# Wider pieces in the conversion of the weights, and softmax chains shared by two token tiles, in a fused attention and soft mixture kernel

## Chip, cores and metric

The kernel runs on one core of one Trainium2 chip. The metric is the device time of one execution in microseconds (us); lower is better. The engines are named as the profile names them: PE (TensorE; its weight loads are a row of their own, PEld), DVE (VectorE), ACT (ScalarE), POOL (GpSimd) and SP, which here only issues DMAs.

## What is computed

Three stages follow each other: an attention with a window of 32 and 32 global tokens, a dense two layer block, and a soft mixture of eight experts.

```
attn_out = attention(q_l, k_l, v_l, q_g, k_g, v_g)     # 4 batches, 8 heads, 512 + 32 rows, 64 wide
x = attn_out.transpose(0, 2, 1, 3).reshape(2176, 512)
h = x @ w_in                                           # 512 x 2048
g = maximum(0.01 * h, h)
x = g @ w_out                                          # 2048 x 512
logits = x @ phi                                       # 512 x 32
d = exp(logits - logits.max(0));  d /= d.sum(0)        # over the tokens
slot_in = d.T @ x
slot_out = per expert: maximum(slot_in @ w1, 0) @ w2
c = exp(logits - logits.max(1));  c /= c.sum(1)        # over the 32 slots
out = c @ slot_out
```

w_in and w_out come as 64 bit floats, so the kernel reads them as pairs of 32 bit words and makes 32 bit floats of them itself.

## The kernel before

The 2176 rows are 17 token tiles of 128 (16 of the local rows, the last of the global ones). x @ w_out is never formed: the kernel makes pmat = w_out @ phi once, so that a tile's logits are g @ pmat, and sums d.T @ g over the tiles (`uacc`); w_out is applied to that sum at the end.

**The conversion.** `w_items` goes through w_in in 16 pieces of 128 x 512 (four column blocks f, four row blocks k), `p_items` through w_out in 16 pieces (c, j). `Stream` keeps raw loads ahead of their use: `fetch` issues a load of 128 x 256 word pairs into a ring of seven buffers, `next` converts the oldest half piece and lets the next load follow. The loads are issued by SP, in order with all its other loads. One `convert` is five instructions: two on ACT (L248 for the high words, L249 for the low ones), two on DVE (L251, L255), and an add on POOL (L259), each 128 x 256, so ten for a piece. A piece of w_in is then split in two parts for the matmuls, by ACT (L307) and by POOL or DVE (L308); its high words pass through PSUM for f > 0 (`cv`). A piece of w_out, in one of four buffers `wo` that w_in's pieces share, is stored to HBM as converted (L337, `wo_f`), and transposed on PE (`chunk`, L344); ACT copies that (L346), and after four chunks `prod` (L353) adds the block's part of pmat. The first nine half pieces of w_out have slots of their own (`spread`, in the attention's tags se, eT and kw); the rest use the ring.

**The token tiles.** `b_H(t, f)` is one 512 column block of h for tile t: 12 matmuls (L688) and an ACT instruction that makes g (L695). Blocks of tiles 0 to 2 run while the weights are converted (`hs`), those of tile 3 (`h3`) after that. Then comes, per tile, the softmax chain that `l_items` lists: transposes of g (`b_L`, L725, evacuated at L727), the logits (`b_M`, L739), their copy (L748), a matmul that brings the four partial sums together (L754), the running maximum (L758, L762), the exponentials (L763), the rescaling of the running sum (L767 to L769), a transpose (L799), the row softmax (`d_rows`, L786 to L794) and the sum over tokens (`u_add`, L809, L814). Each step needs the one before it, and goes from PE to DVE to ACT and back.

**The order.** The statements near L989 run the chain of tile 2, then `merge` lays the chains of tiles 0 and 1 and the rest of tile 3's blocks among the attention of batch 1 (`s4` to `s7`) by the weights beside each item. The chain of tile 3 is laid among the blocks of tile 4 by `b_items`. When the kernel is built, a scheduler orders the instructions of each engine once more; each engine then runs its list in order. From tile 4 on, `b_items` alternates blocks and chains, and the last two tiles have one joint chain (`j_D`) on 256 columns.

## Time and profile before

| what | value |
|---|---|
| median of 3 runs | 515.6 us (515.17 to 520.35) |
| profiled execution | 517.65 us |
| its span | 515.7 us |
| PE busy | 469.5 us (91%) |
| DVE, ACT, POOL busy | 282.1, 240.5, 166.2 us |
| granted PE clock, mean | 0.973 |
| moved by DMA | 90.26 MB, 175 GB/s over the span |

The span is the time from the first to the last recorded instruction; the execution's own time has some 2 us more around it. All stretches and durations below come from this one execution, which took 2.05 us more than the median. "PE busy" holds pipelined matmuls, so a stretch at 91% still has waits in it, and the idle time before an instruction stands apart with what ended it.

### The profile page before, as it was taken

To read this page: it belongs to the slowest core of one execution; us is meant where nothing else is said; L and a number is where in the kernel's file an instruction comes from. 1 tells how busy PE (TensorE), PEld (TensorE's weight loads), DVE (VectorE), ACT (ScalarE), POOL (GpSimd) and SP (SyncE) were. 2 spreads that over 40 slices of the span, in tenths; PEclk is the share of its full clock that TensorE was granted. 3 is DMA by queue.
4 is the path that set the end of the run, shared out by engine and by line. 5 is a ranking of instruction groups with operands and counts; after the bars stand their busy time and mean duration, and the time that the engine had idled before them with its cause. 6 is when DMAs were issued, how large, how long until landed. Compare 5 with 4: busy or idle time off the path is not lost.

```text
span 515.7 us, 13708 instructions
## 1 busy us (share of the span) xinstructions
PE 469.5 (91%) x5327; PEld 324.7 (63%) x5327; DVE 282.1 (55%) x956; ACT 240.5 (47%) x742; POOL 166.2 (32%) x309
## 2 busy tenths in 40 slices
PE   8867798868998979999999979999999999999993
PEld 5645575546775756666767657778677777633353
DVE  4585868659658476565453646534755531312422
ACT  4676888758845345444154254324433442300222
POOL 2044787453301113406233251406666620000000
PEclk9987899997999999999999999999999999999997
DMA  9989679598867471532431203209820059999977
GB/s 173 198 203 242 194 211 335 171 316 251 185 156 151 128 147 25 104 75 76 104 70 35 56 1 57 85 19 394 324 81 2 1 197 344 377 384 378 304 236 209
DMA packets 122397, 90.26 MB, mean 175 GB/s; under 512 B 75804, under 2 KB 101212, under 8 KB 122332
## 3 DMA queue, kind: packets, MB, share of 16 engines
q1 hardware_dynamic: 119660, 88.33, 60.4%
q10 hardware_dynamic: 2672, 1.05, 0.8%
q8 instruction: 42, 0.69, 0.6%
q14 instruction: 23, 0.19, 0.1%
HBM read 76.68 MB, written 8.65 MB: 165 GB/s over the span
## 4 chain that ended last, share of the span: by engine, by line
PE 65%; DMA 14%; DVE 8%; ACT 7%; issue 2%; SPq 2%; POOL 1%; ACTq 0%; DVEq 0%; POOLq 0%
PE hp L688 32%; PE ehp L1177 3%; PE up L809 3%; DMA rraw<-in_moe_w_in_dram 3%; PE po L492 3%; PE sc L433 3%; PE lg L739 2%; DMA vw<-vw 2%; PE gtp L725 2%; DMA rraw<-in_moe_w_out_dram 2%; ACT se L453 2%; DMA vw<-in_v_l_dram 2%; PE etp L472 2%; PE sop L1253 1%; DMA qk<-in_q_l_dram 1%
## 5 line engine op out<-in xcount | busy, mean ns | idle before, releaser
L688 PE MATMUL hp<-wi,xxh 128*128 128x512 f32 x512 | 167.0, 407 | 4.0 <-ACT g L695 2.6
L688 PEld LDWEIGHTS hp<-wi,xxh 128*128 128x128 f32 x512 | 91.9, 190 | 34.8 <-issue 10.6
L716 POOL COPY g<-gb 32x256 f32<-32x256 f32 x206 | 82.5, 400 | 79.3 <-DVE gb L707 66.6
L688 PE MATMUL hp<-wi,xxl 128*128 128x512 f32 x256 | 100.8, 395 | 0.0
L695 ACT ACTIVATE g<-hp 128x512 f32<-128x512 f32 x60 | 35.2, 592 | 66.3 <-PE hp L688 64.4
L453 ACT ACTIVATE se<-se,nmx 128x128 f32<-128x128 f32 x128 | 49.6, 391 | 21.6 <-DVE nmx L451 18.8
L688 PEld LDWEIGHTS hp<-wi,xxl 128*128 128x128 f32 x256 | 48.4, 189 | 11.8 <-issue 0.8
L200 POOL COPY vw<-vw 32x1664 f32<-32x1664 f32 x10 | 15.7, 1574 | 97.7 <-DMA vw<-in_v_g_dram 68.3
L259 POOL TENSOR_TENSOR wn<-wn,rraw 128x256 int32<-128x256 int32 x32 | 26.2, 834 | 37.0 <-DMA rraw<-in_moe_w_in_dram 25.5
L707 DVE STREAM_TRANSPOSE gb<-g 128x512 f32<-128x512 f32 x32 | 22.4, 705 | 23.0 <-ACT g L695 17.7
L445 DVE CUSTOM_DVE_ANT_0 se<-sc,mask 128x128 f32<-128x128 f32 x128 | 28.9, 284 | 7.1 <-PE sc L433 6.9
L433 PE MATMUL sc<-kw,qT 64*32 64x128 f32 x1024 | 29.7, 284 | 0.5 <-DVE kw L404 0.3
L492 PE MATMUL po<-vw,eT 128*32 128x64 f32 x1024 | 23.7, 228 | 6.2 <-DMA vw<-vw 4.7
L259 POOL TENSOR_TENSOR wo<-wo,rraw 128x256 int32<-128x256 int32 x23 | 18.5, 818 | 26.6 <-DMA wo_f<-wo 4.9
L492 PEld LDWEIGHTS po<-vw,eT 128*32 128x32 f32 x1024 | 18.1, 113 | 13.5 <-issue 10.6
L472 PE MATMUL etp<-identr,se 128*128 128x128 f32 x128 | 22.3, 296 | 4.6 <-ACT gT L727 3.3
L249 ACT ACTIVATE rraw<-rraw 128x256 int32<-128x256 uint32 x55 | 23.3, 433 | 5.8 <-DMA rraw<-in_moe_w_in_dram 4.9
L433 PEld LDWEIGHTS sc<-kw,qT 64*32 64x32 f32 x1024 | 19.4, 109 | 8.1 <-issue 4.4
L453 ACT ACTIVATION_READ_ACCUMULATOR se<-se,nmx 128x1 f32 x128 | 24.3, 189 | 0.0
L476 DVE COPY eT<-etp 128x512 f32<-128x512 f32 x28 | 18.8, 686 | 7.0 <-PE etp L472 6.7
L404 DVE COPY kw<-kT 128x672 f32<-128x672 f32 x32 | 19.0, 631 | 5.3 <-ACT kT L393 5.2
L472 PEld LDWEIGHTS etp<-identr,se 128*128 128x128 f32 x128 | 15.3, 148 | 10.3 <-ACT gT L727 4.0
(227 smaller groups left out, 803.3 us busy)
## 6 DMA issues: line engine op xcount, KB each, us to landing
ew<-in_moe_w_dram SPq DMA_DIRECT2D x23, 1024.0 KB, 8.5
rraw<-in_moe_w_in_dram SPq DMA_DIRECT2D x32, 256.0 KB, 3.5
vw<-in_v_l_dram SPq DMA_DIRECT2D x60, 112.0 KB, 3.6
rraw<-in_moe_w_out_dram SPq DMA_DIRECT2D x23, 256.0 KB, 5.3
ew<-in_moe_w_dram SPq DMA_DIRECT2D x9, 512.0 KB, 9.1
ew<-in_moe_w_dram SPq DMA_DIRECT2D x17, 256.0 KB, 5.2
wo_f<-wo SPq DMA_DIRECT2D x16, 256.0 KB, 3.8
vn<-in_v_l_dram SPq DMA_DIRECT2D x4, 1024.0 KB, 6.4
```

The source lines that it names most:

```text
L249: nc.scalar.activation(out=m, in_=lo, func=AF.Copy, scale=2.0 ** -29)
L259: nc.gpsimd.tensor_tensor(out=di, in0=di, in1=m, op=ALU.add)
L404: nc.vector.tensor_copy(kw[:, :, 0:96], src)
L433: last_a[0] = nc.tensor.matmul(bks[e][32 * u:32 * u + 32, P * T:P * T + P], qt[64 * e:64 * e + 64, 32 * U:32 * U + 32], kw[win(U) // (NW / ...
L445: nc.vector.tensor_tensor_reduce(out=s[:, T, :], in0=bk[:, P * T:P * T + P], in1=mask[:, 0 if T == 0 else 2 if T == NT - 1 else 1, :], sca ...
L453: exp_last[0] = nc.scalar.activation(out=s[:, T, :], in_=s[:, T, :], func=AF.Exp, bias=nmx[:, e, T:T + 1], accum_out=sm[:, T, e:e + 1],).ins
L472: last_a[0] = nc.tensor.transpose(pt[:, P * T:P * T + P], es[e][:, T, :], ident).ins
L492: last_a[0] = nc.tensor.matmul(pov[32 * u:32 * u + 32, T, e, :], ets[e][:, 32 * U:32 * U + 32], vw[:, win(U), e, :], start=True, stop=True ...
L688: nc.tensor.matmul(hp, a[:, k, :], w[c][:, k, :], start=(k == 0 and n == 0), stop=(k == KD - 1 and n == 2),)
L695: nc.scalar.activation(out=gs, in_=hp, func=AF.Prelu, alpha=0.01)
L707: nc.vector.transpose(out=gb[:, f % 2], in_=gs)
L716: copy(dst[32 * c:32 * c + 32, :, a], src[32 * a:32 * a + 32, :, c])
```

## The change

1. Raw words are loaded and converted in pieces of 128 x 512. The ring has four buffers of that width in place of seven of half of it; the first eight half pieces of w_out (c = 0) stay 256 wide, in eight slots of their own in place of nine. The shared `wo` buffers become three in place of four, which pays for the larger ring.
2. The chains of tiles 2 and 0, and of tiles 1 and 3, are joined (`pair_items`): the logits of both tiles stand side by side, and the copy, the sum of the parts, the maximum, the exponentials and the rescaling run once on 256 columns. `d_rows` still runs once for each tile; the sums over tokens of both tiles are added up in PSUM and added to `uacc` once.
3. The order around it: the pair (2, 0) is laid among block 2 of tile 3 and the first step of `s5`; the pair (1, 3) and block 3 of tile 3 among the rest of the attention of batch 1. Tile 4's blocks then have no chain among them.

```diff
@@ -225,7 +225,9 @@
 
     raw_last = [None]
 
-    def fetch(pool, src, tag="raw", bufs=7):
+    RING = 4
+
+    def fetch(pool, src, tag="raw", bufs=RING):
         n = src.shape[1]
         raw = pool.tile([P, n] + ([2] if src.dtype == U32 else []), src.dtype, tag=tag, name=tag[:1] + "raw", bufs=bufs)
         raw_last[0] = nc.sync.dma_start(out=raw, in_=src).ins
@@ -277,7 +279,7 @@
 
         def next(self, dst=None, half=None):
             self.start()
-            self.ahead = max(self.ahead - 1, 7) if self.ahead > 7 else self.ahead
+            self.ahead = max(self.ahead - 1, RING)
             r = convert(self.pool, self.raw.pop(0), dst, half)
             return r
 
@@ -290,20 +292,18 @@
     def w_items():
         items = []
         win_s = Stream(st, [
-            w_in_s[P * k:P * k + P, 512 * f + 256 * h:512 * f + 256 * h + 256]
-            for f in range(NQ) for k in range(KD) for h in range(2)
-        ], 7)
+            w_in_s[P * k:P * k + P, 512 * f:512 * f + 512]
+            for f in range(NQ) for k in range(KD)
+        ], RING)
         items.append((0.0, win_s.start))
 
         def piece(f, k):
             if k == 0:
                 wi[f] = [wp.tile([P, KD, 512], F32R, tag="w", name="wi") for _ in range(2)]
             t, tlo = wi[f]
-            w = pb.tile([P, 512], F32, tag="wo", name="wn", bufs=4)
+            w = pb.tile([P, 512], F32, tag="wo", name="wn", bufs=3)
             cv = bank("sc", "cv", 2) if f else None
-            for h in range(2):
-                c = slice(256 * h, 256 * h + 256)
-                win_s.next(w[:, c], cv[:, c] if f else None)
+            win_s.next(w, cv)
             nc.scalar.copy(t[:, k], w)
             (nc.vector if f and k % 2 else nc.gpsimd).tensor_tensor(out=tlo[:, k], in0=w, in1=t[:, k], op=ALU.subtract)
 
@@ -317,12 +317,13 @@
         items = []
         wts = {}
         wout_s = Stream(st, [
-            w_out_s[512 * j + P * c:512 * j + P * c + P, 256 * h:256 * h + 256]
-            for c in range(4) for j in range(4) for h in range(2)
-        ], 7)
+            w_out_s[512 * j + P * c:512 * j + P * c + P, a:z]
+            for c in range(4) for j in range(4)
+            for a, z in (((0, 256), (256, 512)) if c == 0 else ((0, 512),))
+        ], RING)
         def begin():
             with tc.issue_after(raw_last[0]):
-                wout_s.spread([("se", 4)] * 4 + [("eT", 2)] * 2 + [("kw", 3)] * 3)
+                wout_s.spread([("se", 4)] * 4 + [("eT", 2)] * 2 + [("kw", 3)] * 2)
                 wout_s.start()
 
         items.append((0.0, begin))
@@ -330,9 +331,9 @@
         wos = []
 
         def conv_(c, j):
-            wo = pb.tile([P, 512], F32, tag="wo", name="wo", bufs=4)
-            for h in range(2):
-                wout_s.next(wo[:, 256 * h:256 * h + 256])
+            wo = pb.tile([P, 512], F32, tag="wo", name="wo", bufs=3)
+            for h in range(2) if c == 0 else (None,):
+                wout_s.next(wo if h is None else wo[:, 256 * h:256 * h + 256])
             if wo_f is not w_out:
                 nc.sync.dma_start(out=wo_f[512 * j + P * c:512 * j + P * c + P, :], in_=wo)
             wos.append(wo)
@@ -875,6 +876,48 @@
             (1.0, lambda: b_U(t)),
         ]
 
+    def p_M(ts, i):
+
+        if i == 0:
+            ms["M"] = bank("sm", "lg", 1)
+        lg = ms["M"]
+        for f in range(NQ):
+            gT = lst.pop((ts[i], f))
+            for c in range(4):
+                nc.tensor.matmul(
+                    lg[32 * c:32 * c + 32, P * i:P * i + P], pmat[:, c, f, :], gT[:, c, :],
+                    start=(f == 0), stop=(f == NQ - 1), skip_group_check=True,
+                )
+
+    def p_D1(ts):
+        lp = sb.tile([P, 2 * P], F32, tag="lp", name="lp", bufs=1)
+        nc.vector.tensor_copy(lp, ms["M"][:, 0:2 * P])
+        ms["lp"] = lp
+
+    def p_D2(ts):
+        ms["st"] = d_cols(ms["M"][:, 2 * P:4 * P], ms["lp"])
+
+    def p_D3(ts):
+        lg = ms["M"]
+        for i, t in enumerate(ts):
+            nc.tensor.transpose(lg[:, P * i:P * i + P], ms["st"][:, P * i:P * i + P], ident)
+        ms["ds"] = [(d_rows(t, lg[:, P * i:P * i + 64]), gt.pop(t)) for i, t in enumerate(ts)]
+
+    def pair_items(ts):
+        its = []
+        for i, t in enumerate(ts):
+            its += [
+                (0.9, lambda t=t: (b_L(t, 0), b_L(t, 1))),
+                (0.9, lambda t=t: (b_L(t, 2), b_L(t, 3))),
+                (0.6, lambda i=i: p_M(ts, i)),
+            ]
+        return its + [
+            (0.1, lambda: p_D1(ts)),
+            (0.5, lambda: p_D2(ts)),
+            (0.5, lambda: p_D3(ts)),
+            (2.0, lambda: u_add(ms["ds"], ts[-1])),
+        ]
+
     def h_items(t):
         its = [(2.6, lambda f=f: b_H(t, f)) for f in range(NQ)]
         if t + 1 < NTT:
@@ -899,6 +942,9 @@
             li = l_items(t - 1)
             h = [held((1.3, lambda t=t, f=f, a=a: b_H(t, f, a))) for f in range(NQ) for a in range(2)]
             x = [(0.5, lambda t=t: b_X(t + 1), t + 1)] if t + 1 < NTT else []
+            if t == NT:
+                its += h[0:4] + x + h[4:]
+                continue
             if t - 1 in BLK:
                 its += h[0:2] + [li[1]] + h[2:4] + [li[2]] + x + [behind(h[4])]
                 its += [li[3]] + [behind(x) for x in h[5:8]] + [li[4], li[5]]
@@ -986,11 +1032,9 @@
     xb.append(bctx.enter_context(tc.tile_pool(name="xb", bufs=1, side="right")))
     gctx = ExitStack()
     gp.append(gctx.enter_context(tc.tile_pool(name="gp", bufs=1, side="right")))
-    for x in l_items(2):
-        x[1]()
+    merge(pair_items((2, 0)), [h3[2]] + s5[:1])
     load_v(NP + 1)
-    l0, l1 = l_items(0), l_items(1)
-    merge(l0 + h3[2:] + l1, s4[-1:] + s5 + s6 + s7)
+    merge(h3[3:] + pair_items((1, 3)), s4[-1:] + s5[1:] + s6 + s7)
     b_X(NT)
     attn = [None] + [sum((step(n) for n in range(NP * b, NP * b + NP)), []) for b in range(2, B)]
     LB = NTT - 2
```

What the build makes of it stands at three places.

SP's list around the fourth load of values (`vw`; L231 and L233 are the raw loads, L184 and L185 the copies of a window of values within SBUF). Before:

```order
L598 DMA gn<-in_q_g_dram 32x8x64 x4
L962 DMA phis<-in_moe_phi_dram 128x4x32
L231 DMA rraw<-in_moe_w_in_dram 128x512 x3
L184 DMA vw<-vw 32x1792 x2
L185 DMA vw<-vw 32x13x128
```

And now:

```order
L599 DMA gn<-in_q_g_dram 32x8x64 x4
L1008 DMA phis<-in_moe_phi_dram 128x4x32
L233 DMA rraw<-in_moe_w_in_dram 128x1024
L184 DMA vw<-vw 32x1792 x2
L185 DMA vw<-vw 32x13x128
```

One raw load of twice the width stands ahead of the copies, where there were three.

ACT's list at the first pieces of w_out that reuse a `wo` buffer (sraw, eraw, kraw and rraw are raw words; g and wt are evacuations of PE's results). The semaphores DMAHW5 and DMAHW6 before, and DMAHW1 and DMAHW2 now, are those of the first and second store to `wo_f`. Before:

```order
L248 ACTIVATE wo<-kraw 128x256 [waits Pool_49]
L248 ACTIVATE wo<-kraw 128x256
L249 ACTIVATE rraw<-rraw 128x256 [waits DMAHW7_49]
L695 ACTIVATE g_894<-hp 128x512 [waits PE_49]
L346 COPY wt<-wotp 128x512 [waits PE_49]
L249 ACTIVATE rraw<-rraw 128x256 [waits DMAHW0_49]
L249 ACTIVATE rraw<-rraw 128x256 [waits DMAHW1_49]
L249 ACTIVATE rraw<-rraw 128x256 [waits DMAHW2_49]
L249 ACTIVATE rraw<-rraw 128x256 [waits DMAHW3_49]
L695 ACTIVATE g<-hp 128x512 [waits PE_49]
L249 ACTIVATE rraw<-rraw 128x256 [waits DMAHW4_49]
L248 ACTIVATE wo<-kraw 128x256 [waits DMAHW5_49]
```

And now:

```order
L251 ACTIVATE rraw<-rraw 128x512 [waits DMAHW7_49]
L251 ACTIVATE rraw<-rraw 128x512 [waits DMAHW0_49]
L696 ACTIVATE g_860<-hp 128x512 [waits PE_49]
L250 ACTIVATE wo<-kraw 128x256 [waits DMAHW1_49,Pool_49]
L250 ACTIVATE wo<-kraw 128x256
L347 COPY wt<-wotp 128x512 [waits PE_49]
L250 ACTIVATE wo<-rraw 128x512 [waits DMAHW2_49,Pool_49]
L696 ACTIVATE g<-hp 128x512 [waits PE_49]
```

The fourth piece waits for the first store, where the fifth did; the first pair of rows before is the fourth piece, with no such wait.

PE's list around the first chain (lg are logits, st the exponentials, gtp, etp, kTp, qTp transposes, sc, po, gl attention, up the sum over tokens, hp a block of h). Before, from the first to the second matmul L754:

```order
L754 MATMUL lg<-lp,s_77 128x128
L725 MATMUL gtp<-identr,g 128x128 x8
L472 MATMUL etp<-identr,se 128x128 x8
L389 MATMUL kTp<-identr,kn 128x128 x4
L492 MATMUL po<-vw,eT 32x64 x4
L799 MATMUL lg<-identr,st 128x128
L389 MATMUL qTp<-identr,qn 128x128 x4
L492 MATMUL po<-vw,eT 32x64 x13
L809 MATMUL up<-g_894,d 32x512 x4
L492 MATMUL po<-vw,eT 32x64 x6
L739 MATMUL lg<-gT,pmat 32x128 x16
L492 MATMUL po<-vw,eT 32x64 x9
```

And now, the joint one:

```order
L755 MATMUL lg<-lp,s_77 128x256
L390 MATMUL qTp<-identr,qn 128x128 x4
L493 MATMUL po<-vw,eT 32x64 x28
L726 MATMUL gtp<-identr,g 128x128 x4
L434 MATMUL sc_2247<-kw,qT 32x128 x14
L903 MATMUL lg<-identr,st 128x128 x2
L434 MATMUL sc_2247<-kw,qT 32x128 x2
L434 MATMUL sc_2248<-kw,qT 32x128 x16
L726 MATMUL gtp<-identr,g 128x128 x4
L810 MATMUL up<-g_860,d 32x512 x4
L689 MATMUL hp<-wi,xxh 128x512 x2
L689 MATMUL hp<-wi,xxl 128x512
```

One matmul of 256 columns and two transposes stand where there were two rounds, with attention work between them in both lists; the sum of tile 0 follows behind a block of tile 3.

## Rows read from the trace of the kernel before

**Rows 1.** The page, first part: busy time, share, instructions

```profile
PE 469.5 (91%) x5327; PEld 324.7 (63%) x5327; DVE 282.1 (55%) x956; ACT 240.5 (47%) x742; POOL 166.2 (32%) x309
```

**Rows 2.** By stretch: length, five engines (instructions), PEclk, DMA share, GB/s

```profile
20.00:54.00 34.00, 22.97 (x440) 15.79 (x438) 23.02 (x82) 23.56 (x79) 14.41 (x16) 0.85 0.92 216
54.00:98.00 44.00, 39.57 (x184) 29.31 (x185) 34.53 (x77) 36.33 (x95) 33.46 (x38) 0.96 0.70 229
98.00:143.00 45.00, 38.35 (x497) 27.92 (x495) 30.17 (x108) 33.18 (x103) 17.10 (x22) 0.92 0.89 251
143.00:200.00 57.00, 51.69 (x904) 36.81 (x907) 38.72 (x160) 27.23 (x106) 6.29 (x4) 1.00 0.61 127
```

**Rows 3.** Waits of PE, same stretches: total, times, longest

```profile
PE po L492 <- DMA vw<-vw: 4.3, 3, 2.6
...
PE hp L688 <- ACT g L695: 2.9, 3, 1.4
...
PE wotp L344 <- POOL wo L259: 3.4, 2, 3.1
...
PE up L809 <- DVE d L786: 2.3, 2, 1.8
PE lg L754 <- DVE lp L748: 0.5, 1, 0.5
```

**Rows 4.** Timeline of SP's queue around 36 us: start, us, what it issued

```profile
36.08 1.39 SPq L231 DMA_DIRECT2D rraw<-in_moe_w_in_dram  x3
37.52 1.17 SPq L184 DMA_DIRECT2D vw<-vw  x2
```

**Rows 5.** Timeline of ACT: two conversion runs, fifth piece of w_out

```profile
66.37 1.12 ACT L307 CAST wi<-wn 128x512 fp32r<-128x512 f32 x2
...
91.27 1.42 ACT L249 ACTIVATE rraw<-rraw 128x256 int32<-128x256 uint32 x4
93.38 0.42 ACT L248 ACTIVATE wo<-kraw 128x256 f32<-128x256 f32 x1
```

**Rows 6.** Groups by form, 20 to 145 us: busy, mean ns | idle before

```profile
L259 POOL TENSOR_TENSOR wn<-wn,rraw 128x256 int32<-128x256 int32 x32 | 26.2, 834 | 37.0 <-DMA rraw<-in_moe_w_in_dram 25.5 <-DVE wn L255 8.2 <-ACT cv L248 1.1
L308 POOL TENSOR_TENSOR wi<-wn,wi 128x512 fp32r<-128x512 f32 x10 | 13.2, 1326 | 5.4 <-ACT wi L307 4.0 <-DMA rraw<-in_moe_w_in_dram 0.7 <-DMA vw<-in_v_l_dram 0.6
L251 DVE TENSOR_SCALAR cv<-cv 128x256 uint32<-128x256 uint32 x24 | 9.7, 424 | 4.1 <-ACT cv L248 4.0
```

**Rows 7.** Groups by form, 143 to 244 us: 512 column copy, reduction

```profile
L727 DVE COPY gT<-gtp 128x512 f32<-128x512 f32 x9 | 6.1, 681 | 3.9 <-PE gtp L725 2.6 <-PE ptps L359 0.6 <-PE ptps L353 0.6
L758 DVE TENSOR_REDUCE nm<-lg 128x1 f32<-128x128 f32 x5 | 1.4, 284 | 0.7 <-PE lg L754 0.7
```

**Rows 8.** Line L344, transposes of w_out: ns, first and last start

```profile
L344 PE MATMUL wotp<-identr,wo x64: 270/273/476, 86.0 to 142.3; 128*128 128x128 f32 x64
```

**Rows 9.** Timeline of PE: third and eighth piece of w_out transposed

```profile
98.54 0.60 PE L344 MATMUL wotp<-identr,wo 128*128 128x128 f32 x4
...
108.04 0.63 PE L344 MATMUL wotp<-identr,wo 128*128 128x128 f32 x4 [0.49 <-ACT wt L346]
```

**Rows 10.** Timeline of POOL: the fifth piece of w_out, a late copy

```profile
95.78 0.79 POOL L259 TENSOR_TENSOR wo<-wo,rraw 128x256 int32<-128x256 int32 x1
...
187.22 1.57 POOL L200 COPY vw<-vw 32x1664 f32<-32x1664 f32 x1 [16.46 <-DMA vw<-in_v_g_dram]
```

**Rows 11.** Line L337, the stores of converted w_out: time to landing

```profile
DMA to landing us min/median/max: 2.0/3.8/7.5
```

**Rows 12.** Busy time by stretch, behind PE's longest wait for w_out

```profile
114.77:130.00 15.23, 13.74 (x188) 10.53 (x188) 12.95 (x53) 12.39 (x40) 4.92 (x6) 0.78 0.86 242
```

**Rows 13.** Groups by form, 440 to 450 us: the reduction on 256 columns

```profile
L758 DVE TENSOR_REDUCE nm<-lg 128x1 f32<-128x256 f32 x1 | 0.4, 425 | 0.9 <-PE lg L754 0.9
```

**Rows 14.** Timeline of DVE: one small instruction twice

```profile
156.48 0.16 DVE L458 TENSOR_SCALAR sm<-sm 128x8 f32<-128x8 f32 x1
...
187.35 1.48 DVE L458 TENSOR_SCALAR sm<-sm 128x8 f32<-128x8 f32 x1 [0.42 <-ACT se L453]
```

## Prediction

> **What bounds the kernel now.** I read the page first: PE is busy for 91% of the span [rows 1]. What is left to win is PE's idle time, so I went on to busy time by stretch. From 143 us on PE has little air (51.69 of 57.00 us between 143 and 200); the air is ahead of it: 22.97 of 34.00 us, 39.57 of 44.00, 38.35 of 45.00 [rows 2]. The three stretches are the first attention with the start of w_in, the conversion of w_in beside the blocks of tiles 0 to 2, and the conversion of w_out. In the middle one ACT (36.33 us), DVE (34.53) and POOL (33.46) are nearly as full as PE, so none of them alone is the bound; they take turns. Third, I read whom PE waits for in these stretches [rows 3]: for values copied within SBUF (4.3 us), for ACT's evacuation of g (2.9), for POOL's conversion of w_out (3.4, of which 3.1 at once), and, after 143 us, for the chains (2.3 and 0.5). These waits, 13.4 us in all, are what the change can reach; it takes no columns from PE.
>
> **The change part by part.**
>
> *One raw load ahead of the value copies instead of three.* SP spends 36.08 to 37.47 us on three raw loads, and only then issues the copies that PE awaits later [rows 4]. With one load this takes about a third, so the copies go out some 0.9 us earlier: I take -1.0. At best the whole longest wait goes, -2.6 [rows 3]; at worst the copies land when they did, since the same bytes are in flight: 0.
>
> *Half the conversion instructions of w_in.* Back to back, four ACT instructions on 256 columns take 1.42 us, of which the last 0.43 alone, so one adds 0.33; two on 512 columns take 1.12, so one adds 0.51 [rows 5]. High and low words of a piece cost 4 x 0.33 = 1.32 us before and 2 x 0.51 = 1.02 now: 0.30 less on ACT. On DVE a step on 256 columns takes 0.424 [rows 6] and the nearest one on 512, a copy out of PSUM, 0.681 [rows 7]: two steps of a piece save 2 x (0.848 - 0.681) = 0.33. On POOL the add takes 0.834 on 256 columns, and an operation of two inputs on 512 takes 1.326 [rows 6]: 0.34 less. Of the 16 pieces the last 12 run beside the blocks, so each of the three engines gets back 3.6 to 4 us in a stretch of 44. PE sees of that only what it waits for. The 2.9 us for g came in three waits, the longest 1.4 [rows 3], each of them with ACT still at conversions; I take two thirds back, -2.0. The most is all the idle time of the stretch, 44.00 - 39.57 = 4.4 [rows 2]. The other end is a loss: a wide piece passes each engine later than its second half did. One ACT step is 0.18 longer, two DVE steps 0.26 each, POOL 0.49: 1.2 us. If the blocks start when a piece comes through and not when an engine is free, that is +1.2.
>
> *w_out: fewer instructions, but three buffers.* The 16 pieces are transposed from 86.0 to 142.3 us [rows 8], 3.5 us apiece, and in a burst from the third to the eighth, 98.54 to 108.04, every 1.9 us [rows 9]. A buffer is held from ACT's first step to POOL's end (the fifth piece: 93.38 [rows 5] to 95.78 + 0.79 = 96.57 [rows 10], 3.2 us), some 0.4 until SP issues the store, and a landing of 3.8 in the median [rows 11]: 7.4 us. Three buffers come round in 10.5 us at the mean pace, which is enough, but in 5.7 us in the burst: two rounds are late by 1.7 each, 3.4 us. Four buffers had 7.6 us there, just enough. Behind the waiting ACT instruction stand the evacuations of g and of the transposes, and PE waits for those. The burst ran into a wait of 3.1 us [rows 3] before, however, which hides most of the lateness; net I take +0.5. At worst each landing takes the 7.5 us that was the largest [rows 11]: 11.1 against 5.7, two rounds, 10.8 less 3.1 makes +7.7. At best the 3.1 us wait goes, and with it the clock that fell behind it: PE ran at 0.78 granted for 15.23 us [rows 12], 3.4 us at full clock: -6.5.
>
> *Two chains less.* PE waited 2.8 us for the four chains [rows 3]. Joint steps are longer: a maximum over 128 columns takes 0.284 [rows 7], over 256 columns 0.425 [rows 13], so the three steps maximum, exponentials and copy add about 0.4 for a pair, 0.8 in all. Then the transposes of two tiles stand together and want four evacuations in a row; I set 0.5 for that, an estimate from the smaller of the two chain waits. -2.8 + 0.8 + 0.5 = -1.5. DVE also loses two updates of 512 columns, but it is not what PE waits for. The best is -2.8; the worst has both joint chains wait as the longest did, 2 x (1.8 + 0.4) = 4.4, which is +1.6.
>
> *Sum.* -1.0 - 2.0 + 0.5 - 1.5 = -4.0 us: 517.65 becomes 513.65 for the profiled execution. That took 2.05 us more than the median of the runs, so I forecast **511.6 us**, 0.8% under 515.6. A measurement of this kernel tells about 1% (5.2 us) from no change, so this is no clear gain.
>
> **Rivals.**
>
> *The wait for w_out goes with its dip in the clock.* Fewer instructions on ACT, DVE and POOL bring the ninth piece in time, and PE stays at its upper level. For it: the three engines have 30.17, 33.18 and 17.10 us of work in 45 [rows 2], so they were waiting and not full. Against it: the DMA share there is 0.89, and the bytes stay. -1.0 - 2.0 - 6.5 - 1.5 = -11.0: 504.6.
>
> *Coarser pieces win nothing.* The conversion is paced by handing on, not by instructions: -1.0 + 1.2 + 0.5 - 1.5 = -0.8: 514.8. For it: POOL idles for 8.2 us of its adds to w_in waiting on DVE [rows 6]. Against it: ACT is busy 83% there.
> A POOL instruction also holds up DVE: one on 8 columns took 0.16 us alone and 1.48 beside a POOL copy of 1.57 us [rows 10, 14]. The Trainium skill, "SBUF — State Buffer", section "SBUF: two separate sides", says that the two engines share a pair of ports that is locked for a whole instruction, so that the loser blocks until it ends; the trace agrees with 1.48 for 0.16. By that rule a wide add blocks a DVE step for up to 1.33 us and not 0.83, this rival loses 0.5 more, and the time would be 515.3.
>
> *Slower: the stores set the pace.* The place is ACT's wait for a store at the fourth piece of w_out and on. If landings are near 7.5 us, because wider raw loads stand ahead of the stores in the same queue, the stage loses 7.7, and a second long wait brings a second dip of the clock, another 3.4: -1.0 - 2.0 + 7.7 + 3.4 - 1.5 = +6.6: 522.2. It decides from a landing of about 6 us on, where two rounds lose 7.8, twice what I reckoned. Against it: the median was 3.8.
>
> **How the numbers follow.** Forecast 0.42, the long wait gone 0.20, nothing won 0.23, stores 0.15. The forecast's own range is 508 to 516.5, and some of it lies beyond 1%: 0.15 of its 0.42 faster, 0.27 same. The first rival is faster (0.20); nothing won is the same but for 0.02 (0.21); the stores are slower (0.15). Faster 0.35, same 0.48, slower 0.17. The range 504.0 to 519.5 leaves out the lower part of the first rival, about 0.07, and most of the last, about 0.12.
>
> **What would show it.** Right: the copies of values issued about 1 us earlier near 36 us; PE's wait for g between 54 and 98 us under 1.5 us; PE's waits on chains after 143 us near 1.3; the first full block of tile 4 about 4 us earlier. In ACT's waits a store to `wo_f` appears by name. Wrong: a wait for w_out of over 3 us with the granted clock low behind it in two places (stores), or none at all (first rival); idle time of PE between 54 and 98 us that stays near 4.4 (nothing won); a chain wait after 143 us longer than 2.2, which the last term leaves no room for.

## The result, and the profile after

The changed kernel takes 497.25 us in the median of 4 runs (496.2 to 500.06), beside 517.98 for the kernel before on the same chip, with a ratio of 0.964 and an interval of [0.960, 0.969]. The kernel before is slower in some executions (520.4 us), and ratios compare the fast executions alone, so that they are not the quotient of two medians. A second measurement gave 497.65 and 0.967 [0.963, 0.971]. Forecast were 511.6 and a range of 504.0 to 519.5: faster it is, but by 3.6% and not 0.8%. The profiled execution took 496.2 us, with a span of 494.5; before it was 517.65 and 515.7.

The page's first part, which answers [rows 1]:

```profile
PE 463.5 (94%) x5323; PEld 322.0 (65%) x5323; DVE 275.0 (56%) x886; ACT 234.3 (47%) x680; POOL 160.3 (32%) x281
```

PE's busy time fell by 6 us (some of it ran at the lower clock before), its idle time by 15. The busy times by stretch tell where; the first four rows answer [rows 2], in the same columns, and the last is the piece that ends with a chain's matmul L755 at 291.8 us, which as L754 stood at 312.5 us before:

```profile
20.00:54.00 34.00, 24.46 (x443) 17.56 (x442) 23.97 (x73) 24.52 (x69) 15.49 (x12) 0.79 0.89 224
54.00:98.00 44.00, 42.08 (x211) 31.19 (x210) 31.54 (x53) 34.20 (x71) 30.07 (x25) 0.97 0.75 252
98.00:143.00 45.00, 41.53 (x614) 30.91 (x614) 33.25 (x109) 34.58 (x99) 13.39 (x10) 1.00 0.86 247
143.00:200.00 57.00, 55.32 (x905) 37.53 (x904) 39.12 (x144) 25.19 (x90) 10.81 (x15) 1.00 0.59 119
...
143.00:292.00 149.00, 147.32 (x2216) 104.40 (x2215) 89.89 (x344) 65.39 (x230) 46.34 (x89) 1.00 0.42 89
```

The same view of the kernel before, for that last piece:

```profile
143.00:312.00 169.00, 159.09 (x2339) 112.62 (x2346) 97.89 (x381) 71.70 (x257) 46.34 (x89) 1.00 0.40 85
```

Three gains are to be read here. Between 54 and 98 us PE is busy 2.5 us longer. Between 98 and 143 it is busy 3.2 us longer, and its granted clock is 1.00 where it was 0.92, which is 45 x 0.08 = 3.6 us of full clock: 6.8 together. Behind 143 us PE idled 169.00 - 159.09 = 9.9 us before and 149.00 - 147.32 = 1.7 now: 8.2. The first stretch ends 1.2 us earlier (the first block of h starts at 53.54, before at 54.72); 0.7 us of that lies behind 54 us and is in the 2.5 already. The sum is 18.0 of the 21.2 us that the span lost; the rest is spread over the remainder.

Whom PE waits for in these stretches, as in [rows 3]:

```profile
PE po L493 <- DMA vw<-vw: 1.4, 2, 0.9
...
PE hp L689 <- ACT xqn L665: 1.9, 1, 1.9
PE hp L689 <- ACT xxh L665: 1.2, 1, 1.2
...
PE gtp L726 <- DVE gT L728: 1.3, 1, 1.3
PE wotp L345 <- POOL wo L261: 0.7, 1, 0.7
...
PE get L561 <- DVE get L563: 1.0, 1, 1.0
```

The waits for g (2.9 us before) and for chains behind 143 us (2.8) are gone, that for POOL's w_out is 0.7 us where it was 3.4. One wait for a chain, the 1.3 us for DVE's evacuation of transposes (`gtp`), now stands ahead of 143 us; it ends at 141.05.

The conversion's first and last transposition of w_out, beside [rows 8]:

```profile
L345 PE MATMUL wotp<-identr,wo x64: 270/273/329, 81.0 to 137.7; 128*128 128x128 f32 x64
```

It begins 5.0 us earlier than before and ends 4.6 us earlier. This line turned out to be the best gauge of all the kernels below.

### The profile page after: what moved, and what is told of

It is laid out like the page before. It is cut to its first block, busy times and chain, and to the rows that moved or that the text cites. A ratio compares the mean times of both kernels' runs of the same rounds, so it can differ in the third digit from the quotient of the medians.

```text
span 494.5 us, 13438 instructions
## 1 busy us (share of the span) xinstructions
PE 463.5 (94%) x5323; PEld 322.0 (65%) x5323; DVE 275.0 (56%) x886; ACT 234.3 (47%) x680; POOL 160.3 (32%) x281
## 4 chain that ended last, share of the span: by engine, by line
PE 78%; DVE 4%; ACT 4%; DMA 1%; issue 1%; POOL 0%; ACTq 0%; DVEq 0%; POOLq 0%
PE hp L689 38%; PE gtp L726 4%; PE ehp L1221 3%; PE sc L434 3%; PE up L810 3%; PE po L493 3%; PE lg L740 2%; PE etp L473 2%; PE sop L1297 2%; PE sop L1275 1%; PE gpo L579 1%; PE wotp L345 1%; PE qTp L390 1%; PE kTp L390 1%; PE xtp L659 1%; PE gl L519 1%
## 5 line engine op out<-in xcount | busy, mean ns | idle before, releaser
L261 POOL TENSOR_TENSOR wn<-wn,rraw 128x512 int32<-128x512 int32 x16 | 22.8, 1435 | 34.5 <-DVE wn L257 33.0
L261 POOL TENSOR_TENSOR wo<-wo,rraw 128x512 int32<-128x512 int32 x12 | 16.0, 1332 | 31.7 <-DVE wo L257 7.2
L251 ACT ACTIVATE rraw<-rraw 128x512 int32<-128x512 uint32 x28 | 18.7, 673 | 4.3 <-DMA rraw<-in_moe_w_out_dram 3.1
```

The source lines that it names most:

```text
L261: nc.gpsimd.tensor_tensor(out=di, in0=di, in1=m, op=ALU.add)
```

## The experiments

Seventeen kernels follow from the two, and the changed one ran again: each undoes or does one part. Ratios are to the kernel before on the same chip; "over the changed kernel" means over its 497.65 us, the median of its second measurement (the kernels ran on four chips, on which the median of the kernel before lay between 515.1 and 516.5).

**The two halves.** The first kernel has the diff's hunks on `fetch`, `Stream`, `w_items` and `p_items` alone, the second the others.

> Part 1 alone: raw words in a ring of four 512 column pieces, three `wo` buffers, conversion steps on 512 columns; the softmax chains and their order are those of the kernel before. Read from the two traces, the changed kernel gains about 11 of its 21 us before the end of the w_out conversion and about 10 after it. Theory (the two parts add, each paid in its own stretch): about 11 us under the kernel before, 507, with the long wait of PE for a piece of w_out gone and the granted clock at 1.0 from 98 to 143 us. Rival 1 (the early finish of the conversion is all of it, the later gains follow from it): about 498. Rival 2 (the order of blocks and chains does it, the conversion's width does not): 515 to 518, with the long wait still there.

Measured: 516.1 us, ratio 1.003 [0.9995, 1.007].

> Parts 2 and 3 alone: joint chains of tiles (2, 0) and (1, 3), their order and tile 4's blocks without a chain; the conversion on 256 columns with the ring of seven and four `wo` buffers, as before. Theory (the parts add): about 9 to 10 us under the kernel before, 508, with the long wait for w_out still there. Rival 1 (all is the conversion): 515 to 518. Rival 2 (all is the order): about 498.

Measured: 509.3 us, ratio 0.985 [0.977, 0.994]; PE's longest wait for w_out is still 2.0 us.

The halves don't add up: no change and 1.5% make 3.6% together. The wide ring alone has its longest wait for w_out down to 1.2 us and the clock at 0.98 between 98 and 143 us, so the conversion does what the first theory says, and its last transposition comes 3.0 us earlier (139.3 for 142.3); but its gain isn't paid out. What takes it stands right behind:

```profile
128.00:150.00 22.00, 18.16 (x281) 13.22 (x280) 11.42 (x40) 12.72 (x36) 3.87 (x3) 0.92 0.50 133
```

The kernel before has PE busy for all 22.00 us there, at a clock of 0.96. Where its conversion still gives PE work, the wide ring leaves 3.8 us idle.

**Which part of the conversion.** In the changed kernel, the steps of both weights, of w_in, or of the last 12 pieces of w_out are done in two halves on a wide load. The first of the three edits:

```diff
-            r = convert(self.pool, self.raw.pop(0), dst, half)
-            return r
+            raw = self.raw.pop(0)
+            n = raw.shape[1]
+            for a in range(0, n, 256):
+                c = slice(a, a + 256)
+                convert(self.pool, raw[:, c], dst[:, c], half[:, c] if half is not None else None)
+            return dst
```

> The changed kernel with 512 column loads in its ring of four, but every conversion step done in two halves of 256 columns. It tells apart the number of instructions on ACT, DVE and POOL from the width of the loads and the depth of the ring. If the number of instructions is what the conversion gained: about 8 us over the changed kernel, 505. If it is the loads (fewer issues on SP, one wait for a piece, eight half pieces ahead instead of seven): within 2 us of the changed kernel, 497 to 499.

Measured: 504.9 us, ratio 0.978 [0.971, 0.984].

> The changed kernel itself, on the same chip as the three runs beside it, so that they can be compared with it and not only by way of the kernel before. Expected: ratio to the kernel before again 0.960 to 0.970.

Measured: 497.65 us, ratio 0.967 [0.963, 0.971].

> The changed kernel with the conversion steps of w_in alone done in two halves of 256 columns (loads stay wide). Both weights in halves cost 7.7 us, and by the traces all of it came behind 89 us. Theory 1 (the steps of w_out are what matters): within 1.5 us of the changed kernel. Theory 2 (w_in done early lets w_out begin early, which is what carries the later stage): 4 to 8 us over it, with the first transpose of w_out several us after the changed kernel's 81.0.

Measured: 504.6 us, ratio 0.980 [0.974, 0.987], 7.0 over the changed kernel.

> The changed kernel with the conversion steps of the last 12 pieces of w_out alone done in two halves. Theory 1: 6 to 8 us over the changed kernel, with the granted clock under 0.9 from 98 to 143 us. Theory 2: 0 to 3 us over it.

Measured: 499.7 us, ratio 0.970 [0.966, 0.976], 2.1 over it, with a granted clock of 1.00 from 98 us on.

The second theory holds: w_in's steps matter, though the loss shows only at w_out. With narrow steps on w_in, busy time by stretch, PE's waits from 98 to 143 us, and the transpositions read:

```profile
54.00:98.00 44.00, 43.23 (x212) 32.21 (x211) 32.52 (x73) 36.38 (x90) 29.75 (x35) 0.94 0.70 227
98.00:143.00 45.00, 35.90 (x500) 26.92 (x500) 29.97 (x88) 30.27 (x80) 14.67 (x11) 0.96 0.89 262
```

```profile
PE wotp L350 <- POOL wo L261: 4.4, 7, 0.9
PE ptps L359 <- ACT wt L352: 2.0, 2, 1.7
```

```profile
L350 PE MATMUL wotp<-identr,wo x64: 271/273/331, 85.6 to 142.8; 128*128 128x128 f32 x64
```

Up to 98 us PE does the work that it does in the changed kernel (212 matmuls to 211; that it is busy 43.23 us and not 42.08 goes with the lower clock): the blocks cover everything. Then they are used up, w_out is 4.6 us behind, and PE is busy 35.90 us where it was 41.53, with seven waits for POOL and two for ACT in between. What an engine saves while another covers it is not lost; it comes due where the cover ends.

**The ring's depth and the `wo` buffers.** `RING = 3`, with four `wo` buffers or three; then four buffers beside the ring of four (`phis` in the tag st, `xg` in the tag geg); then the narrow conversion with `bufs=8` and three `wo` buffers; then `RING = 5` with `kw` in two buffers.

> The changed kernel with four `wo` buffers and a ring of three wide pieces, in the same space. In the prediction three `wo` buffers cost PE up to 3.4 us, of which 0.5 net. If the stores still hold up ACT in the changed kernel: 494 to 496. If raw words ahead are worth more than buffers behind: 499 to 505, with PE or ACT waiting for raw loads. If neither is tight: 496 to 498.5.

Measured: 509.8 us, ratio 0.987 [0.980, 0.993].

> The changed kernel with a ring of three wide pieces and three `wo` buffers, which leaves 4 KB a partition unused. The run with a ring of three and four `wo` buffers lost 12 us of the 20. If the depth of the ring is what counts: again 508 to 511. If the fourth `wo` buffer did the harm (by letting the conversion run ahead into other work): 497 to 500. If it takes both: between.

Measured: 510.4 us, ratio 0.991 [0.987, 0.996].

> The changed kernel with its ring of four wide pieces and four `wo` buffers, for which room is made by two small tiles that share the space of others (phi's rows with the exponentials of the chains, the global values with their transposes). The runs with a ring of three lost 12 to 13 us, with three or four `wo` buffers alike. Theory (the fourth `wo` buffer is worth little, since ACT hardly waits for the stores in the changed kernel): 496 to 498.5, no difference. Rival (the stores do hold up ACT, as the prediction had it): 493 to 495.5.

Measured: 500.5 to 510.0 us in six executions, median 506.6, ratio 0.978 [0.971, 0.986]. None was faster than the changed kernel. The new home of the small tiles changes the order too, and the scatter leaves open what the buffer itself does.

> Joint chains and the new order with 256 column loads and steps, but a ring of eight and three `wo` buffers, the bytes of the changed kernel. With a ring of seven and four `wo` buffers this kernel stood at a ratio of 0.985; with wide loads in a ring of four and narrow steps at 0.978. If the eighth half piece ahead made that difference: 0.976 to 0.980. If the wide loads did (one issue and one wait for two): 0.983 to 0.988.

Measured: 506.9 us, ratio 0.985 [0.979, 0.990].

> The changed kernel with a ring of five wide pieces, for which the attention's key windows (`kw`) have two buffers in place of three. A ring of three lost 13 us against four. If depth still binds at four and the third `kw` buffer is worth nothing: 492 to 495. If four is enough: 496 to 499. If the missing `kw` buffer holds up the attention, which then waits for key windows: 500 to 506.

Measured: 511.1 us, ratio 0.993 [0.989, 0.997].

Depth counts: with three wide pieces the changed kernel loses 12 to 13 us, whatever the number of `wo` buffers. What ACT waits for from 54 to 143 us in the kernel with a ring of three and three buffers:

```profile
ACT cv L250 <- DMA rraw<-in_moe_w_in_dram: 5.9, 6, 1.9
```

and in the changed kernel:

```profile
ACT rraw L251 <- DMA rraw<-in_moe_w_out_dram: 3.1, 2, 3.0
...
ACT cv L250 <- DMA rraw<-in_moe_w_in_dram: 1.9, 4, 0.6
...
ACT rraw L251 <- DMA rraw<-in_moe_w_in_dram: 1.2, 1, 1.2
```

For loads of w_in that is 5.9 us against 3.1; the changed kernel's wait for a load of w_out has no like in the other. The first transposition of w_out comes at 88.9 us with a ring of three (81.0 with four), though its first block of h starts at 51.0 us (53.5). An eighth half piece gains nothing when the pieces are narrow (0.985 either way); whether the wide loads make the difference to narrow steps on wide loads (0.978) is not settled, since the intervals overlap. With five pieces w_out begins early (80.1 us), but the attention is late: the first block of h starts at 57.8 us, and PE waits 3.6 us for `xqn` and 3.3 for `xn` between 54 and 98 us. That is later than the third branch of the expectation had it, and its cause is not shown: PE waits only 1.5 us for key windows ahead of 54 us (0.4 in the changed kernel). Whether a fifth piece by itself helps stays open.

**The order.** Chains apart at the new places (`l_items(2) + l_items(0)` and `l_items(1) + l_items(3)` for the pairs); the pair (2, 0) alone; the block's new place without the rest, on the wide ring alone; tile 3's chain back; the new order on the kernel before.

> The changed kernel with the chains of tiles 2, 0, 1 and 3 apart again (128 columns each, as before), laid at the same places in the order: 2 and 0 beside block 2 of tile 3, 1 and 3 beside the attention, tile 4's blocks without a chain. Theory (the place of blocks and chains gains, the joining hardly does): within 3 us of the changed kernel, 497 to 501, and no wait of 3 us near 300 us. Rival (the two chains saved are the gain): 504 to 509, with waits of PE for chains of over 2 us between 140 and 230 us.

Measured: 499.75 us, ratio 0.974 [0.970, 0.978].

> The changed kernel, but the pair (2, 0) stands alone behind the conversion, as tile 2's chain did before; block 2 of tile 3 and the first step of the next attention come after it. Theory (the block of tile 3 fills PE's waits at the end of the conversion): 4 to 6 us over the changed kernel, 501 to 504, with idle time of PE of some 4 us more between 128 and 150 us. Rival (the joining does it, the block's place does not): 497 to 499.

```diff
-    merge(pair_items((2, 0)), [h3[2]] + s5[:1])
+    for x in pair_items((2, 0)):
+        x[1]()
...
-    merge(h3[3:] + pair_items((1, 3)), s4[-1:] + s5[1:] + s6 + s7)
+    merge(h3[2:] + pair_items((1, 3)), s4[-1:] + s5 + s6 + s7)
```

Measured: 503.3 us, ratio 0.981 [0.977, 0.984], 5.7 over the changed kernel.

> The kernel with the wide ring alone and the old chains, with one thing from the new order: block 2 of tile 3 and the first step of the next attention laid beside tile 2's chain. The wide ring alone was 8 us ahead of the kernel before at the end of the w_out conversion and gave 5 of them back between 132 and 147 us. Theory (that block fills the end of the conversion): 4 to 6 us under the wide ring alone, ratio to the kernel before 0.990 to 0.995. Rival (the joint chain is needed for it): no better than the wide ring alone, ratio 1.00.

Measured: 518.6 us, ratio 1.008 [1.004, 1.012]. The theory fell: the block alone doesn't rescue the wide ring. It does fill the place that it was meant for; the loss comes behind it. Busy time there, and in the 50 us that follow:

```profile
128.00:150.00 22.00, 20.07 (x288) 14.98 (x287) 10.58 (x36) 11.55 (x35) 3.90 (x3) 0.92 0.44 120
150.00:200.00 50.00, 44.94 (x737) 29.61 (x730) 31.86 (x133) 21.35 (x83) 6.30 (x4) 0.93 0.54 112
```

The wide ring alone has 45.61 us busy from 150 to 200 at a clock of 1.00. A likely reason, which no run tests apart: the block that was moved forward is missing in that attention, and tile 3's chain, which stands there in the changed kernel, is still among the blocks of tile 4.

> The changed kernel with one piece of the order undone: tile 3's chain stands again among the blocks of tile 4, tile 1's chain alone beside the attention of batch 1; the pair (2, 0) stays joint at its new place. Theory (tile 3's chain gives PE work in the gaps of batch 1's attention, and tile 4's blocks without it shift the next attention so that the wait of 3 us near 300 us goes): 8 to 12 us over the changed kernel, 505 to 509, with that wait back and PE's busy share between 150 and 230 us lower. Rival (block 2 of tile 3 and the joint pair carry the order's gain): within 3 us of the changed kernel.

```diff
-            if t == NT:
-                its += h[0:4] + x + h[4:]
-                continue
...
-    merge(h3[3:] + pair_items((1, 3)), s4[-1:] + s5[1:] + s6 + s7)
+    merge(h3[3:] + l_items(1), s4[-1:] + s5[1:] + s6 + s7)
```

Measured: 512.6 us, ratio 0.994 [0.989, 0.998], 15 over the changed kernel: the direction of the theory, and more than its 8 to 12. Of the 15, 2.4 stand ahead of the last transposition of w_out (140.1 us for 137.7), before the chain that was moved.

> The kernel before with the new order alone: four separate chains at the new places, the conversion on 256 columns, nothing joined. Parts 2 and 3 together gave 1.5% (7.5 us). Theory (the place, not the joining): ratio to the kernel before 0.983 to 0.990, within 3 us of parts 2 and 3 together. Rival (joining is the larger half): ratio 0.993 to 1.000.

Measured: 508.3 us, ratio 0.989 [0.982, 0.996], beside 0.985 with the chains joint. The two intervals overlap widely, and the medians stand the other way round (508.3 and 509.3).

The places are worth nearly all, and a worth of the joining is not shown. The kernel with the chains apart is 2.1 us slower than the changed one, but it has lost 2.2 us by the first transposition of w_out (83.2 us for 81.0), before any chain. From the first block of h to there PE's instructions stand in the same order in both. 0.6 us is a first block that starts later (54.18 us); behind it the clock falls after a wait for `xqn` that both kernels have. From 60 to 70 us, with the chains apart:

```profile
60.00:70.00 10.00, 8.30 (x30) 6.16 (x30) 7.59 (x11) 8.19 (x15) 9.49 (x7) 0.83 0.79 232
```

and in the changed kernel:

```profile
60.00:70.00 10.00, 8.08 (x51) 5.95 (x50) 8.17 (x12) 9.37 (x19) 8.99 (x8) 1.00 0.84 230
```

Block 2 of tile 3, with the first step of the next attention, fills the end of the conversion. Busy time of the kernel whose pair stands alone, up to that point and behind it:

```profile
98.00:128.00 30.00, 28.25 (x409) 20.89 (x408) 26.08 (x80) 25.25 (x72) 9.45 (x7) 1.00 1.06 303
128.00:150.00 22.00, 18.71 (x280) 13.26 (x274) 9.48 (x33) 10.32 (x30) 3.88 (x3) 0.84 0.44 116
```

and of the changed kernel:

```profile
98.00:128.00 30.00, 28.28 (x408) 20.95 (x408) 26.10 (x81) 25.38 (x71) 9.54 (x8) 1.00 1.05 302
128.00:150.00 22.00, 20.19 (x303) 14.94 (x303) 10.44 (x35) 10.97 (x31) 3.85 (x3) 1.00 0.41 113
```

Up to 128 us they are the same; then 1.5 us of idle time and a clock of 0.84 (22 x 0.16 = 3.5 us) make the loss. Tile 3's chain does the same for the attention of batch 1. Busy time of the kernel that has it late, and three rows of PE's timeline:

```profile
150.00:230.00 80.00, 73.31 (x1152) 49.92 (x1149) 52.94 (x204) 34.67 (x130) 16.14 (x23) 0.98 0.49 102
```

```profile
192.04 1.11 PE L473 MATMUL etp<-identr,se 128*128 128x128 f32 x4 [2.12 <-ACT gT L728]
...
213.20 0.66 PE L726 MATMUL gtp<-identr,g 128*128 128x128 f32 x4 [1.82 <-ACT kT L394]
...
297.28 0.66 PE L473 MATMUL etp<-identr,se 128*128 128x128 f32 x4 [2.75 <-ACT gT L728]
```

The changed kernel is busy 78.38 us between 150 and 230, 5.1 more, and has none of the three waits. The chain's transposes and logits need nothing of batch 1, so they are work for PE while that attention goes round by DVE and ACT. The wait near 300 us is in every kernel with tile 3's chain among the blocks of tile 4 (3.02 us before, 3.01 in the wide ring alone), and in no other.

**What is left.** Of PE's idle time in the changed kernel, 9.5 us stand between 20 and 54 us; from 54 to 400 us there are 7.5. The fillers `warm` were doubled at three places there, or taken out:

> The changed kernel with two filler matmuls where it has one, ahead of the scores, the transposes of the exponentials and the weighted values of the first batch's attention (they write a bank that is overwritten, and keep PE busy while it has nothing to do). After 54 us PE idles some 7 us in all in the changed kernel; between 20 and 54 us it idles 9.5, and its granted clock is 0.79. If that clock holds up the first attention: 493 to 496, with a higher clock there. If the first attention waits for other engines and loads, PE's clock does not matter: 496 to 499. If the fillers stand in the way: over 499.

Measured: 506.8 us, ratio 0.980 [0.977, 0.983].

> The changed kernel without those fillers (the ones ahead of the transposes of queries and keys stay). If the clock matters there: 498 to 502, at a lower granted clock from 20 to 54 us. If it does not: 495 to 498.

Measured: 506.6 us, ratio 0.980 [0.977, 0.984].

With fillers doubled the clock came up where it was meant to, and nothing was gained by it. Busy time by stretch of that kernel, and its blocks of h:

```profile
20.00:54.00 34.00, 23.37 (x456) 16.72 (x454) 22.50 (x68) 22.54 (x67) 13.16 (x10) 0.95 0.92 214
98.00:143.00 45.00, 38.60 (x464) 28.56 (x463) 27.36 (x88) 29.83 (x78) 13.01 (x10) 0.81 0.81 242
```

```profile
L692 PE MATMUL hp<-wi,xxh x512: 387/392/797, 56.0 to 433.2; 128*128 128x512 f32 x171
```

The first block of h starts at 56.0 us where it was 53.5, w_out's first transposition is at 84.8, and from 98 to 143 us PE stands waiting at a clock of 0.81. So the time is that of the third branch of its expectation, and a higher clock did not bring the first block forward. Whether the fillers themselves stand in the way, or the order that the build made around them, no run tells apart. The kernel without them missed both of its numbers; its first block starts at 55.0 us at a granted clock of 0.85 from 20 to 54, and why it then loses 9 us is open. No kernel here beats the changed one. Part of that may be the build: every edit has the scheduler order the whole program anew. The order alone edits nothing ahead of the conversion's end, and yet its first block of h starts 2.9 us earlier than in the kernel before (51.8 us for 54.7). A difference of 2 or 3 us between two kernels is therefore not by itself the worth of the part in which they differ; the larger ones rest on where the trace shows the loss.

**All kernels in one table.** The last transposition of w_out (line L345 or its like), the profiled execution, and what lies between, in us, from one execution of each:

| kernel | last transposition | execution | between |
|---|---|---|---|
| before | 142.3 | 517.65 | 375.4 |
| wide ring alone | 139.3 | 515.27 | 376.0 |
| the same, block beside tile 2's chain | 139.1 | 519.85 | 380.8 |
| changed, tile 3's chain late | 140.1 | 514.55 | 374.5 |
| joint chains and order alone | 143.2 | 510.29 | 367.1 |
| order alone | 140.3 | 507.32 | 367.0 |
| changed, pair alone | 137.2 | 503.08 | 365.9 |
| **changed** | **137.7** | **496.2** | **358.5** |
| chains apart | 139.9 | 499.94 | 360.0 |
| w_out's steps narrow | 139.1 | 499.62 | 360.5 |
| w_in's steps narrow | 142.8 | 504.79 | 362.0 |
| all steps narrow | 145.3 | 506.94 | 361.6 |
| narrow, ring of eight | 144.6 | 507.26 | 362.7 |
| ring of three | 148.3 | 508.43 | 360.1 |
| ring of three, four `wo` | 148.2 | 509.00 | 360.8 |
| ring of five, two `kw` | 150.2 | 509.73 | 359.5 |
| ring of four, four `wo` (one of its longer executions) | 147.2 | 509.63 | 362.4 |
| fillers doubled | 148.5 | 508.77 | 360.3 |
| no fillers | 140.5 | 503.55 | 363.1 |

The last column falls into groups: 374 to 381 with tile 3's chain late, 358 to 363 with the whole new order, and 366 to 367 where the block of tile 3 doesn't fill the end of the conversion, or where (the order on the narrow conversion, chains joint or not) PE waits 2.2 us at once for values behind 143 us. Within the new order the time follows the end of the conversion. So the change did two things: it ended the conversion 4.6 us earlier, and it shortened what follows by 16.9. Why the conversion ends so late with a ring of five and with doubled fillers, though it begins at 80 and 85 us there, is not settled beyond the low clock seen there.

## Why the prediction was right and wrong

*One load ahead of the value copies: -1.0, right in size, not shown in cause.* SP's queue, beside [rows 4]:

```profile
35.25 0.44 SPq L233 DMA_DIRECT2D rraw<-in_moe_w_in_dram  x1
35.74 1.17 SPq L184 DMA_DIRECT2D vw<-vw  x2
```

The copies go out 1.8 us earlier, 0.95 of it by the two loads fewer; PE's wait for them fell from 4.3 to 1.4, and the first block starts 1.2 us earlier. But the kernel with joint chains and order alone, which still has the three loads there, issues its copies as early:

```profile
34.00 1.39 SPq L231 DMA_DIRECT2D rraw<-in_moe_w_in_dram  x3
35.45 1.17 SPq L184 DMA_DIRECT2D vw<-vw  x2
```

Its first block starts at 53.7 us, and that of the order alone, with three loads too, at 51.8. So the number came out, but no run shows that the single load brought it; that part is luck as far as is known.

*Half the instructions of w_in: the sizes right, the reckoning wrong.* The steps, beside [rows 6]:

```profile
L261 POOL TENSOR_TENSOR wn<-wn,rraw 128x512 int32<-128x512 int32 x16 | 22.8, 1435 | 34.5 <-DVE wn L257 33.0 <-ACT rraw L251 0.6 <-ACT wi L307 0.4
...
L253 DVE TENSOR_SCALAR cv<-cv 128x512 uint32<-128x512 uint32 x12 | 8.3, 692 | 2.5 <-ACT cv L250 2.5
L257 DVE SCALAR_TENSOR_TENSOR wn<-rraw,cv 128x512 uint32<-128x512 uint32 x12 | 8.1, 681 | 0.3
...
L257 DVE SCALAR_TENSOR_TENSOR wo<-rraw,wo 128x512 uint32<-128x512 uint32 x12 | 8.3, 692 | 0.3
```

DVE's two steps take 1.37 us (1.36 reckoned), POOL's add 1.435 where two took 1.67: 0.23 saved and not 0.34. The wide add did not hold up DVE more than narrow ones do, at least not in the mean: its wide steps cost what a copy of that width costs. Of the longer block of the second rival, and of its price of 0.5, these rows show nothing. The Trainium skill ("SBUF — State Buffer", section "SBUF: two separate sides") limits that lock to a VectorE instruction in a 2-port mode or with two inputs from SBUF. The rival passed over that; the steps of w_in shown have one operand in PSUM (`cv`), and the step of w_out with both in SBUF (`wo<-rraw,wo`) takes 0.692 us too. PE got 2.5 us back between 54 and 98 us, 1.8 without the earlier first block, where the forecast had 2.0. The step that failed is "PE sees of that only what it waits for", with its ceiling of 4.4 us taken from that stretch: it made the rest of the saved engine time worthless. It went on to w_out instead: w_out began 5.0 us earlier, and undoing w_in's part alone costs 7.0 us in all, with the first transposition back at 85.6 us (86.0 before the change).

*w_out: +0.5, wrong; on this term the first rival had the size.* The lateness for want of buffers did not come: no store stands among ACT's waits, and the time to landing, beside [rows 11], was

```profile
DMA to landing us min/median/max: 2.0/3.2/6.2
```

The long wait went, and the dip of the clock with it: 6.8 us of busy time and clock, where the rival had 6.5. Its reason, fewer instructions, holds for w_in's more than for w_out's own: those in halves cost only 2.1 us, with the clock still at 1.00. The prediction also took the long wait for POOL's alone; ACT's first step of that piece had itself waited for a raw load:

```profile
110.51 0.44 ACT L248 ACTIVATE wo<-rraw 128x256 f32<-128x256 f32 x1 [1.22 <-DMA rraw<-in_moe_w_out_dram]
```

The rival's whole sum, -11.0, had a chance of 0.20; what spoke against it, that "the bytes stay" and the DMA share was 0.89, was no reason, since that share is still 0.86. Right was that this wait and the clock go together.

*Two chains less: -1.5, wrong by the most.* The term was built from the waits that the view puts down to chains, 2.8 us, and "PE has little air" behind 143 us passed over what has no name there. The idle time from 143 to 312 us was 9.9 us before, the wait of 3.0 near 300 among it; 8.2 of it went. And the third point of the change, the order, had no term at all, as if work that is moved cost the same anywhere. By the runs the joining, which the term was for, has no worth that is shown; tile 3's chain beside the attention is worth some 13 us (15 less the 2.4 ahead of it), the block and the attention's first step at the end of the conversion 6. These are what undoing one part costs, and they are not to be added: they overlap.

*The range.* It ended at 504.0, inside the first rival. Even the best cases of the four terms together (-2.6 - 4.4 - 6.5 - 2.8 = -16.3) give 499.3, above what was measured. The first rival's 504.6 had kept the small term for the chains; with the 8.2 in its place it would have given 497.9.

*The signals.* Copies earlier: yes. Wait for g under 1.5 us: it is gone. Chain waits near 1.3 behind 143 us: there are none, but one of 1.3 just ahead of it. A store among ACT's waits: none. First full block of tile 4 about 4 us earlier: it begins at 186.73 us and not at 195.15, 8.4 us earlier, though tile 3's chain now stands ahead of it.

## What to carry to other kernels

Idle time that no wait names is still idle time: take the ceiling of a change from the stretch's busy share, and ask what independent work could stand there. Time saved on an engine that is covered by another is handed on to where the cover ends; follow the producer to its last piece (here the last transposition), because within one order the time followed it here. Two halves of a change can each be worth little and much together: here one moved the end of a stage, and the other had work for the gap that this opened and for the attention behind it. And before a few us between two builds are put down to an edit, look where in the trace the loss begins; 2 us that seemed to be the joining's began ahead of every chain.

## What the runs showed of the hardware

The granted clock behind a wait is not told by the wait alone. PE waited 3.0 us for ACT near 300 us in the kernel before and in the wide ring alone. The 7 us from the end of that wait, before:

```profile
302.00:309.00 7.00, 6.98 (x76) 4.98 (x76) 3.35 (x7) 2.24 (x4) 6.04 (x15) 1.00 0.01 2
```

and in the wide ring alone:

```profile
298.00:305.00 7.00, 6.68 (x49) 4.82 (x50) 2.83 (x5) 1.76 (x4) 5.74 (x15) 0.76 0.01 2
```

The clock stayed at its upper level in the one and fell in the other, with 49 matmuls recorded in the time of 76. The rows from 60 to 70 us above show it with PE's instructions in the same order: behind a wait of 1.9 us for `xqn` the changed kernel stays at 1.00, behind one of 1.7 us the kernel with its chains apart falls to 0.83. Behind 60 us, up to its last matmul, the changed kernel has no such stretch at all, and of the kernels that are 7 us or more behind it all but one show a clock under 1.00 between 98 and 150 us; the one, with tile 3's chain late, has its dips near 65, 190 and 300 us.
